# First block of a spectral filter: direct products on array quarters, halved start products, and a new order of the first loads and weight conversions

## The chip, the cores and the metric

The kernel runs on one core of a Trainium2 chip. The metric is the device time of one execution in microseconds (us). Three runs of the kernel before took 2608.47, 2609.06 and 2609.44 us, a median of 2609.06. PE is the matmul engine, DVE the vector engine (VectorE), ACT the scalar engine (ScalarE), POOL is GpSimd and SP the engine that issues most transfers.

## The reference

Eight sequences of 3008 tokens with 256 channels are filtered along the sequence in the frequency domain, and every token then goes through a two-layer network with a hard swish. `moe_w_in` and `moe_w_out` come as 64-bit floats, the rest as 32-bit floats.

```python
X = np.fft.rfft(x, axis=1)
Y = X * (filt_r + 1j * filt_i)[None, :, :]
y = np.fft.irfft(Y, n=3008, axis=1)
h = y.reshape(8 * 3008, 256) @ w_in            # 256 x 2048
g = h * np.clip(h + 3.0, 0.0, 6.0) / 6.0
out = g @ w_out                                # 2048 x 256
```

## The kernel before

**The filter.** 3008 is 47 x 64, and the transform is done in two stages of small products: over the 47 rows `a` for each of 64 columns `j` (stage a), then over the columns for each of 24 values `k` of the first frequency index (stage b). `f_unit` multiplies by the filter on VectorE (L561 to L563, three operations, one input of each in PSUM), `y_unit` forms real and imaginary sums (L572, L573, all in SBUF), `bi_unit` transforms back over the columns, and its results `t` are stored to the DRAM buffer `g_tmp` (`g_store`, on GpSimd's queue) and loaded again into `t4` in another layout. `n_five`, `n_unit` and, for the first block of tokens, `n_first` transform back over the rows into the ring `xn`.

**The network.** Tokens go in 47 blocks of 512 (`PAIRS` is 256: a token and its mirror image are handled as a pair), and each block takes 8 steps `p` over the hidden width. Block 0 runs plainly (`plain_up`, `plain_down`, L873 to L890); the later ones use sums of seven products, for which GpSimd forms sums of the weights (`w_sums`, L369) while block 0 runs. `relu` (L813) is on ScalarE and `hswish` (L818) on VectorE.

**The weights.** Each of 16 parts of 512 KB arrives as 64-bit words (`load_bits`, L317). `w_abs` on ScalarE (L323, L324) makes the absolute high words and floats of the low words; `w_conv` (L333, L335, L337) and `w_conv_2` (L354, L358, L361) on VectorE make 32-bit floats of them. Without `w_abs` VectorE does two operations more (L340, L349). Part 0 is converted during `a0_unit`, parts 1 to 3 are put around `n_first`, and the others, in halves, into the steps of block 0.

**The opening**, L984 to L1081, is written out by hand, and every engine keeps this order:

- SP loads sequence 0 (`x0_load`, six pieces), with the bits of part 0 after the first three of them; then filter table 0, the bits of part 1 and tables 1 to 5 (`table_load`, five transfers each, 768 KB in all); then the tables `direct` and `edge` and the bits of parts 2 and 3. `wi`, which `bi_unit` needs, goes over ScalarE's queue.
- `a0_unit`, eight times: four columns and both channel halves, eight full 112x128 by 112x128 products (L421), of whose 128 result columns 96 are used. The results are copied by ScalarE and VectorE.
- For c = 0 to 5: `b_unit` and `f_unit` for `i = 2c` and `2c + 1`, `turn(c + 1)` (transposes), `bi_unit(2c - 2)` and its store. `i` counts pairs of `k`.
- The last four `k` (units 10 and 11) are not loaded into `t4` for block 0. `direct` takes their part straight from `y`: 16 products in all (four `k`, two channel halves, two banks) over full 128 rows, against a table of 564 columns (two mirror halves of 47 for each of 6 column groups). Unit 8 is stored first by `g0_first` (L625), which takes only the rows that block 0 needs, and in full after `n_first`. `first_load` brings `k` 0 to 11 into `t4` (L663, when c is 4) and then `k` 12 to 19.
- `n_first` adds the rest into the same PSUM banks, 12 products of 94 columns in two strips each (through `strips`, L765), and ScalarE copies the result to `xn` (L741, L744, L745). Then `plain_up(0)` begins.

Tiles rotate. Those that matter here: units 0, 4 and 8 and the `y` of the last units take turns in the two `t1` buffers, so the copies of unit 8 wait until unit 4's store has landed; units 2, 6 and 10 share one `t3` buffer.

Of the kernel before, what the change touches and what calls it, by code (L numbers as in the profile page):

```python
# [27 lines left out]
NA = 47  # L28
# [27 lines left out]
ND = (NJ + 1) * TOK  # L56
NX = PAIRS - NJ * NA
# [21 lines left out]
def _make_tables():  # L79
# [65 lines left out]
    def first_of(x, n):  # L145
        if n < NJ:
            return np.concatenate(x)
        return np.concatenate([x[0][:NX], x[1][:NX], cs_of([x[0][NX:], x[1][NX:]])])

# [4 lines left out]
    first = np.zeros((P, NJ + 1, TOK))  # L154
    last = np.zeros((P, NJ + 1, TOK))
    direct = np.zeros((P, TC, ND))
    for k in range(KH):
        for j in range(HC):
            for (ri, hh), x in terms(k, j, rows).items():
                if j in FIRST:  # L160
                    first[hh * 64 + ri * 32 + k, FIRST.index(j)] = first_of(x, FIRST.index(j))
                if j < 2:
                    ones[ri * ATOM + hh * KH + k, j] = cs_of(x)
# [3 lines left out]
            if j > 1:  # L167
                c, s = (terms(k, j, rows)[0, hh][0] for hh in range(2))
                for hh, v in enumerate((c, s)):
                    groups[hh * KH + k, j] = groups[HALF + hh * KH + k, j] = v  # L170
        if k >= KH - TC:
            for q in range(64):
                fr = k + NA * q if q < 32 else NA * (q - 31) - k
                for n, j in enumerate(FIRST):
                    th = [2 * np.pi * ((fr * rows(j, h, a)) % N) / N for h in range(2)]
                    direct[q, k - KH + TC, n * TOK:(n + 1) * TOK] = 2 / N * first_of(np.cos(th), n)
                    direct[HALF + q, k - KH + TC, n * TOK:(n + 1) * TOK] = -2 / N * first_of(np.sin(th), n)
    wai = np.concatenate([t.reshape(P, -1) for t in (groups, ones, first, last)], axis=1)
# [5 lines left out]
def kernel(  # L184
# [22 lines left out]
    g_d = nc.dram_tensor("g_tmp", (B, NC, 2, KH, D), FP32, kind="Internal").ap()  # L207

# [99 lines left out]
    def w_load(i, q):  # L308
        if W_AT[i] == "g":
            t = gp.tile([P, 7, 256], FP32, name="g")  # L310
            st["rest"] = t[:, 4:7, :].rearrange("p a n -> p (a n)")
# [8 lines left out]
    def w_abs(i):  # L320
        words = st["bits", i].rearrange("p (n two) -> p n two", two=2)
        st["high", i] = sp.tile([P, 512], FP32, name="s1")
        nc.scalar.activation(out=st["high", i], in_=words[:, :, 1].bitcast(FP32), func=AXT.Abs)  # L323
        nc.scalar.activation(out=words[:, :, 0].bitcast(FP32), in_=words[:, :, 0].bitcast(mybir.dt.uint32), func=AXT.Copy, scale=2.0 ** -32)  # L324


    def w_conv(i):
# [11 lines left out]
        if ("high", i) not in st:  # L339
            v.tensor_scalar(out=lo, in0=lo, scalar1=9, scalar2=0x3F800000,  # L340
                            op0=ALU.logical_shift_right, op1=ALU.bitwise_or)

# [74 lines left out]
    def a0_unit(j):  # L417
        for dh in range(2):
            ps = bank(0)
            for u in range(4):  # L420
                nc.tensor.matmul(ps[:, ts(u, P)], x0[0:XR, j + u, ts(dh, P)], st["start"][0:XR, ts(1, P)],  # L421
                                 start=True, stop=True)
            copy(dh and j not in (8, 12), zt(dh).rearrange("p (n j) -> p j n", j=HC)[:, j:j + 4, :],
# [197 lines left out]
    def g0_first(i):  # L621
        t = st["t3", 0, i]
        for v in range(2):
            for h in range(2):
                (nc.scalar, nc.sync)[v].dma_start(g_d[0, ds(h * HC + 1, NJ + 1), :, ds(2 * (i + v), 2), :].rearrange("c ri u d -> c ri (u d)"),  # L625
                                    t[ds(v * 64 + h * HC + 1, NJ + 1)].rearrange("p ri u d -> p ri (u d)"))
# [32 lines left out]
    def first_load(k0, k1):  # L659
        for h in range(2):  # L660
            for ri in range(2):
                p0 = h * 64 + ri * 32
# [59 lines left out]

    def direct(i):
        if "psn" not in st:
            st["psn"] = {(c, dh): (psO.tile([P, 2, 2, P], FP32, name="po%d" % (2 + dh)).rearrange("p a u m -> p (a u m)")
                                   if c else psF.tile([P, 512], FP32, name="psn", tag="f"))
                         for c in range(2) for dh in range(2)}
        for u in range(2):
            k = 2 * i + u - KH + TC
            for (c, dh), ps in st["psn"].items():  # L730
                t, n = c * NJ * TOK, (1 if c else NJ) * TOK
                nc.tensor.matmul(ps[:, 0:n], st["y", 0, i][:, u, ts(dh, P)], st["direct"][k][:, ds(t, n)],
                                 start=k == 0, stop=False, skip_group_check=True)

    def n_first():
        for (c, dh), ps in st.pop("psn").items():
            for q, j in enumerate(chunks[c][1]):
                strips(ps[:, ts(q, TOK)], t4[:, j - 1, ts(dh, P)], edges[:, FIRST.index(j), :], start=False, stop=True)
            to = xn[:, dh, :, 0:PAIRS]
            if c == 0:  # L740
                nc.scalar.activation(out=to[:, :, 0:NJ * NA].rearrange("p h (j a) -> p j h a", a=NA),  # L741
                                     in_=ps[:, 0:NJ * TOK].rearrange("p (j h a) -> p j h a", j=NJ, h=2), func=AXT.Copy)
                continue
            nc.scalar.activation(out=to[:, :, NJ * NA:], in_=ps[:, 0:2 * NX].rearrange("p (h a) -> p h a", h=2), func=AXT.Copy)  # L744
            nc.scalar.activation(out=xn[:, dh, :, ds(PAIRS, NA - NX)],  # L745
                                 in_=ps[:, 2 * NX:TOK].rearrange("p (c a) -> p c a", c=2), func=AXT.Copy)
# [233 lines left out]
    with tc.manual_schedule():  # L980
# [42 lines left out]
        nc.scalar.dma_start(wi, wi_d)  # L1023
# [7 lines left out]
        for j, n, bits in (0, 4, 0), (4, 4, 0), (8, 8, 1), (16, 8, 1), (24, 4, 1), (28, 4, 1):  # L1031
            x0_load(j, n)
            load_bits(bits)
        table_load(0, 0)
        load_bits(2)
        table_load(0, 1)
        for j in range(0, HC, 4):
            a0_unit(j)
            convert(j == 4)
        nc.gpsimd.memset(t4, 0.0)  # L1040
# [249 lines left out]
```

## Time and profile before

| | us |
|---|---|
| median of three runs | 2609.06 |
| profiled execution, first to last instruction (span) | 2607.0 |
| median of the runs above the span | 2.06 |
| PE busy | 2591.8 (99%) |
| VectorE busy | 2053.9 (79%) |
| ScalarE busy | 1295.6 (50%) |
| GpSimd busy | 486.7 (19%) |

The profiled execution's own time is known by its span; what lies outside of it is taken from the timed runs. The granted clock of PE is 1.000 in the mean. Some places of the opening, from the timeline and the records of transfers:

| what | us |
|---|---|
| first and last product of `a0_unit` begin | 6.6 to 21.8 |
| first `f_unit` begins | 25.36 |
| last `y_unit` ends | 54.65 |
| stores of units 0, 2, 4 and 6 issued | 33.3, 38.0, 42.65, 48.5 |
| bits of part 3 (last of the first loads) landed | 50.16 |
| `direct` on PE | 51.13 to 59.7 |
| last load of `first_load` landed | 61.53 |
| first product of `n_first`, of `plain_up(0)`, of `plain_up(1)` | 61.62, 64.22, 68.55 |
| VectorE's conversion of part 3 begins, idles, goes on | 62.36, 64.03, 65.64 |

How to read it: in the timeline a line has start, length, engine, line of the kernel, operation, what is written and read, and in square brackets how long the engine stood idle before it and what ended that. In the groups the number after the bar is busy time, then the mean ns of one instruction, then idle time. The slices cut the span into 40 pieces of 65 us, in tenths busy. The chain of waits gives start, length and what ran. One product of 32-bit floats is two weight loads and two matmul instructions, so ten products in two strips are 40 instructions.

### The profile page before, as it was taken

The numbers are of one execution on the slowest core, as the hardware profiler recorded it, in microseconds if no ns is written. First come the engines' busy times: TensorE is split into PE (matmuls) and PEld (weight loads), VectorE is DVE, ScalarE is ACT, GpSimd is POOL, SyncE is SP. The second block draws the span as 40 slices with busy tenths as digits, with TensorE's granted clock in tenths as the row PEclk, the third lists the DMA queues.
The fourth block names the chain that finished last, engine by engine and source line by source line (L and its number), as shares of the span: only waits on it lengthen the run. The fifth ranks groups of instructions, "written<-read, shape, count | busy, mean of one in ns | idle before, by whom it ended". The sixth has DMA issues, their size and how long they took to land.

```text
span 2607.0 us, 86613 instructions
## 1 busy us (share of the span) xinstructions
PE 2591.8 (99%) x37708; PEld 2051.0 (79%) x37708; DVE 2053.9 (79%) x3611; ACT 1295.6 (50%) x2677; POOL 486.7 (19%) x711
## 2 busy tenths in 40 slices
PE   8999999999999999999999999999999999999999
PEld 6487777878778787788877888777877778888887
DVE  7978868888788877888778887788877888766666
ACT  4554454545545455444554444545445454455554
POOL 2242021121211202111031210311113120111110
PEclk9999999999999999999999999999999999999999
DMA  8732234112241132411224112331123321110000
GB/s 247 224 92 81 59 101 119 54 33 87 74 123 54 33 87 78 119 54 37 83 83 114 54 38 82 89 108 54 54 66 91 106 57 49 50 44 24 20 22 26
DMA packets 130834, 200.32 MB, mean 77 GB/s; under 512 B 21602, under 2 KB 97472, under 8 KB 130262
## 3 DMA queue, kind: packets, MB, share of 16 engines
q1 hardware_dynamic: 115165, 150.12, 20.4%
q0 software_dynamic: 14720, 44.16, 6.1%
q8 instruction: 296, 4.85, 0.8%
q14 instruction: 84, 0.69, 0.1%
q10 hardware_dynamic: 569, 0.50, 0.1%
HBM read 122.43 MB, written 83.98 MB: 79 GB/s over the span
## 4 chain that ended last, share of the span: by engine, by line
PE 94%; DVE 3%; DMA 2%; POOL 1%; issue 0%; ACT 0%; SPq 0%; POOLq 0%; DVEq 0%; ACTq 0%
PE po L765 43%; PE al L765 24%; PE be L765 18%; PE psn L705 2%; PE psf L540 1%; PE psf L481 1%; PE psf L600 1%; PE be L600 1%; POOL w_all L369 1%; PE be L481 1%; DVE g L818 1%; DMA g_tmp<-t 1%; PE psf L765 0%; DMA ft<-in_filt_i_dram 0%; DVE y L335 0%
## 5 line engine op out<-in xcount | busy, mean ns | idle before, releaser
L765 PEld LDWEIGHTS po<-w_all,g 128*64 128x64 f32 x20808 | 1232.5, 137 | 247.0 <-issue 12.4
L765 PE MATMUL po<-w_all,g 128*64 128x128 f32 (+1 forms) x20808 | 1407.0, 274 | 1.4 <-DVE g L818 0.7
L813 ACT ACTIVATE r<-h,half_c 128x512 f32<-128x512 f32 x736 | 531.0, 722 | 346.7 <-DVE h L794 334.7
L765 PE MATMUL al<-xt,w_all 128*64 128x256 f32 x4416 | 664.0, 379 | 0.4 <-POOL w_all L369 0.3
L818 DVE SCALAR_TENSOR_TENSOR g<-r,h 128x512 f32<-128x512 f32 x736 | 536.2, 730 | 144.6 <-ACT r L813 129.2
L765 PE MATMUL be<-xt,w_all 128*64 128x256 f32 x2944 | 442.6, 379 | 0.0
L794 DVE TENSOR_TENSOR h<-be,s 128x512 f32<-128x512 f32 x368 | 253.8, 690 | 131.3 <-PE be L765 102.2
L760 POOL TENSOR_TENSOR xt<-xn 128x256 f32<-128x256 f32 x184 | 150.7, 838 | 890.3 <-ACT xn L687 890.3
L765 PEld LDWEIGHTS be<-xt,w_all 128*64 128x64 f32 x2944 | 211.3, 137 | 106.5
L765 PEld LDWEIGHTS al<-xt,w_all 128*64 128x64 f32 x4416 | 278.9, 137 | 1.7 <-POOL w_all L369 1.4
L808 ACT ACTIVATE h<-al 128x256 f32<-128x256 f32 x368 | 141.4, 384 | 273.2 <-PE al L765 272.4
L826 DVE TENSOR_TENSOR g<-g 128x512 f32<-128x512 f32 x367 | 261.4, 712 | 12.6
L799 DVE TENSOR_TENSOR h<-al,s 128x256 f32<-128x256 f32 x368 | 156.0, 424 | 135.6 <-PE al L765 130.5
L789 ACT ACTIVATE s<-al 128x256 f32<-128x256 f32 x368 | 141.6, 385 | 207.2 <-PE al L765 207.1
L765 PE MATMUL al<-xn,w_all 128*64 128x256 f32 (+1 forms) x1536 | 240.1, 393 | 1.1 <-DVE g L818 0.7
L765 PE MATMUL be<-xn,w_all 128*64 128x256 f32 (+1 forms) x1536 | 236.4, 388 | 0.0
L780 ACT ACTIVATE s<-be 128x256 f32<-128x256 f32 x368 | 141.4, 384 | 170.1 <-PE be L765 170.1
L825 DVE TENSOR_TENSOR g<-g 128x256 f32<-128x256 f32 x367 | 165.5, 451 | 12.6
L779 ACT ACTIVATE s<-al 128x256 f32<-128x256 f32 x368 | 141.5, 384 | 59.1 <-PE al L765 59.1
L831 DVE TENSOR_TENSOR g<-g 128x256 f32<-128x256 f32 x367 | 161.7, 441 | 2.4
L765 PEld LDWEIGHTS be<-xn,w_all 128*64 128x64 f32 x1536 | 110.3, 137 | 62.3 <-issue 7.4
L506 POOL DMA_DIRECT2D z_tmp<-t x144 | 72.0, 508 | 321.4 <-ACT s L780 296.0
(162 smaller groups left out, 1766.6 us busy)
## 6 DMA issues: line engine op xcount, KB each, us to landing
t<-g_tmp SPq DMA_DIRECT2D x184, 120.0 KB
t<-z_tmp SPq DMA_DIRECT2D x42, 512.0 KB
g_tmp<-t POOLq DMA_DIRECT2D x68, 256.0 KB, 4.3
z_tmp<-t POOLq DMA_DIRECT2D x120, 144.0 KB, 3.7
o_tmp<-o SPq DMA_DIRECT2D x46, 256.0 KB
xs<-in_x_dram SPq DMA_DIRECT2D x60, 192.0 KB
ft<-in_filt_r_dram SPq DMA_DIRECT2D x168, 64.0 KB
ft<-in_filt_i_dram SPq DMA_DIRECT2D x168, 64.0 KB
```

What stands on the lines that cost most here:

```text
L760: nc.gpsimd.tensor_tensor(out=o, in0=x0, in1=x1, op=op_)
L765: nc.tensor.matmul(ps[ds(o, STRIP)], w[:, ds(o, STRIP)], x, skip_group_check=True, **kw)
L779: nc.scalar.activation(out=s[:, 0, :], in_=al, func=AXT.Copy)
L780: nc.scalar.activation(out=s5, in_=be[:, 1, :], func=AXT.Copy)
L789: nc.scalar.activation(out=s[:, 1, :], in_=al, func=AXT.Copy)
L794: nc.vector.tensor_tensor(out=st["h"][0].rearrange("p (a n) -> p a n", a=2), in0=be, in1=s, op=ALU.add)
L799: nc.vector.tensor_tensor(out=st["h"][1][:, 256:512], in0=al, in1=s5, op=ALU.add)
L813: nc.scalar.activation(out=r, in_=st["h"][i], func=AXT.Relu, bias=half_c, scale=1.0 / 6.0)
L818: nc.vector.scalar_tensor_tensor(out=st["g", k, p][:, o:o + 2, :].rearrange("p a n -> p (a n)"), in0=st["r", i], scalar=1.0, in1=st["h"][i ...
L825: v.tensor_tensor(out=g[:, G1, :], in0=g[:, G3, :], in1=g[:, G22, :], op=ALU.add)
L826: v.tensor_tensor(out=g[:, G3:G2 + 1:2, :], in0=g[:, G3:G1 + 1, :], in1=g[:, G11:G11 + 1, :].broadcast_to([P, 2, 256]), op=ALU.subtract)
L831: nc.vector.tensor_tensor(out=g[:, G4, :], in0=g[:, G12, :], in1=g[:, G2, :], op=ALU.subtract)
```

## The change

It has five parts, all before block 0 or in it.

1. `a0_unit` computes 96 instead of 128 columns, in two strips of 64 weight columns. VectorE now copies every second group.
2. On SP, all of x comes first, then tables 0 and 1, bits 0, `wi` (moved from ScalarE's queue), tables 2 and 3, bits 1, tables 4 and 5, then the tables of `direct` and `n_first` and bits 2 and 3.
3. Parts 0 and 1 are converted at c = 1 and c = 3: `w_abs` on ScalarE, the first half on VectorE and the second half, four operations, on GpSimd (`w_conv_2g`), ahead of the stores of units 0 and 4 in GpSimd's queue. Part 2 comes ahead of `n_first`, part 3 after it.
4. `direct` and `n_first` compute even and odd sums: real and imaginary rows are separate 64-row products of 47 instead of 94 columns per group, on four quarters of the array. Sum and difference are taken by VectorE in `n_first`. The table has 282 columns for each `k` (564 KB for four instead of 1128 KB), and `n_first` reads the six column groups of `groups` that it needs (141 KB, loaded ahead of the rest of `wai`) instead of a table `first` of its own (282 KB), which goes.
5. Units 6 and 8 go to block 0 through a DRAM buffer of their own, `gf_tmp` (`gf_store`, `gf_load`); unit 6 is stored to `g_tmp` as well, unit 8 as before after `n_first`. Only the part of `t4` that block 0 reads is cleared.

```diff
+NE = (NJ + 1) * NA
...
-            if j > 1:
+            if j:
...
+                    th = 2 * np.pi * ((fr * rows(j, 0, a)) % N) / N
+                    direct[q, k - KH + TC, n * NA:(n + 1) * NA] = 2 / N * np.cos(th)
+                    direct[HALF + q, k - KH + TC, n * NA:(n + 1) * NA] = 2 / N * np.sin(th)
...
+    gf_d = nc.dram_tensor("gf_tmp", (2, HC + NJ + 1, 2, TC, D), FP32, kind="Internal").ap()
...
-    def w_abs(i):
+    def w_abs(i, early=False):
         words = st["bits", i].rearrange("p (n two) -> p n two", two=2)
-        st["high", i] = sp.tile([P, 512], FP32, name="s1")
+        st["high", i] = rp.tile([P, 512], FP32, name="r", tag="r") if early else sp.tile([P, 512], FP32, name="s1")
...
+                             scale=2.0 ** (-52 if early else -32))
...
+    def w_conv_2g(i):
+        big, rest, lo, _ = st.pop(("conv", i))
+        rest, big, high, g = rest.bitcast(FP32), big.bitcast(FP32), st.pop(("high", i)), nc.gpsimd
+        two = lambda t: t.rearrange("p (a d) -> p a d", a=2)
+        g.tensor_tensor(out=rest, in0=lo.bitcast(FP32), in1=rest, op=ALU.mult)
+        g.tensor_tensor(out=rest, in0=rest, in1=big, op=ALU.add)
+        g.tensor_scalar(out=high, in0=high, scalar1=1.125 * 2.0 ** -15, scalar2=None, op0=ALU.is_ge)
+        g.tensor_tensor(out=w_part(i)[1], in0=two(high), in1=two(rest), op=ALU.mult)
...
-                nc.tensor.matmul(ps[:, ts(u, P)], x0[0:XR, j + u, ts(dh, P)], st["start"][0:XR, ts(1, P)],
-                                 start=True, stop=True)
-            copy(dh and j not in (8, 12), zt(dh).rearrange("p (n j) -> p j n", j=HC)[:, j:j + 4, :],
+                strips(ps[:, ds(u * P, 4 * KH)], x0[0:XR, j + u, ts(dh, P)], st["start"][0:XR, ds(P, 4 * KH)],
+                       start=True, stop=True)
+            copy(dh, zt(dh).rearrange("p (n j) -> p j n", j=HC)[:, j:j + 4, :],
...
+    def gf_store(i, qs):
+        t = st["t3", 0, i]
+        for v in range(2):
+            qs[v].dma_start(gf_d[i // 2 % 2, :, :, ds(2 * v, 2), :].rearrange("c ri u d -> c ri (u d)"),
+                            t[ds(v * 64 + 1, HC + NJ + 1)].rearrange("p ri u d -> p ri (u d)"))
+
+    def gf_load(i, qs):
+        for h in range(2):
+            for ri in range(2):
+                qs[h].dma_start(t4[ds(ri * HALF + h * KH + 2 * i, TC), 0:NJ + 1, :],
+                                gf_d[i // 2 % 2, ds(h * HC, NJ + 1), ri, :, :].rearrange("j k d -> k j d"))
...
+    def quarters(ps, dh, w, x, **kw):
+        for g in range(2):
+            for c in range(2):
+                nc.tensor.matmul(ps(c, dh)[ts(g, HALF)], w(c, ds(dh * P + g * HALF, HALF)), x(c), **kw)
+
     def direct(i):
...
+            for dh in range(2):
+                quarters(lambda c, dh: ps[c][dh][:, 0:NE], dh, lambda c, m: y[ts(c, HALF), u, m],
+                         lambda c: st["direct"][ts(c, HALF), ts(k, NE)], start=k == 0, stop=False, skip_group_check=True)
 
     def n_first():
...
+        for dh in range(2):
+            for q, j in enumerate(FIRST):
+                quarters(lambda c, dh: ps[c][dh][:, ts(q, NA)], dh, lambda c, m: t4[ds(c * HALF, ATOM), j - 1, m],
+                         lambda c: groups[ds(c * HALF, ATOM), j, :], start=False, stop=True, skip_group_check=True)
+            e, o = (xn[:, dh, c, :] for c in range(2))
+            odd = ps[1][dh]
+            nc.scalar.activation(out=e[:, 0:NE], in_=ps[0][dh][:, 0:NE], func=AXT.Copy)
+            nc.vector.tensor_tensor(out=o[:, 0:PAIRS], in0=e[:, 0:PAIRS], in1=odd[:, 0:PAIRS], op=ALU.add)
+            nc.vector.tensor_tensor(out=e[:, 0:PAIRS], in0=e[:, 0:PAIRS], in1=odd[:, 0:PAIRS], op=ALU.subtract)
+            nc.scalar.activation(out=o[:, PAIRS:NE], in_=odd[:, PAIRS:NE], func=AXT.Copy)
...
-        nc.scalar.dma_start(wi, wi_d)
...
-        for j, n, bits in (0, 4, 0), (4, 4, 0), (8, 8, 1), (16, 8, 1), (24, 4, 1), (28, 4, 1):
+        for j, n in (0, 4), (4, 4), (8, 8), (16, 8), (24, 4), (28, 4):
             x0_load(j, n)
-            load_bits(bits)
         table_load(0, 0)
-        load_bits(2)
         table_load(0, 1)
+        load_bits(1)
+        nc.sync.dma_start(wi, wi_d)
         for j in range(0, HC, 4):
             a0_unit(j)
-            convert(j == 4)
-        nc.gpsimd.memset(t4, 0.0)
+        nc.gpsimd.memset(t4[:, 0:NJ + 1, :], 0.0)
         for c in range(FB, NT):
             table_load(0, c)
...
+            load_bits(1 + (c > FB))
+        st["direct"] = x0_at(HC * D - 2048, TC * NE)
+        nc.sync.dma_start(st["direct"], direct_d.rearrange("p k n -> p (k n)"))
+        nc.sync.dma_start(wai[:, NA:NA + NE], wai_d[:, NA:NA + NE])
         load_bits(3)
...
+            if c in (1, 3):
+                w_abs(done, True)
+                w_conv(done)
+                w_conv_2g(done)
+                done += 1
             if c + 1 < NT:
                 turn(c + 1)
             if c:
                 bi_unit(0, 2 * c - 2)
-                (g0_first if c == NT - 1 else lambda i: g_store(0, i))(2 * c - 2)
-            if c == 4:
+            if c == NT - 2:
+                gf_store(NU - 6, (nc.sync, nc.sync))
+                g_store(0, NU - 6)
                 first_load(0, KH - 3 * TC)
-        first_load(KH - 3 * TC, KH - TC)
-        for i in 1, 2:
-            w_abs(i)
+            elif c == NT - 1:
+                gf_store(NU - 4, (nc.sync, nc.scalar))
+            elif c:
+                g_store(0, 2 * c - 2)
+        gf_load(NU - 6, (nc.sync, nc.sync))
+        gf_load(NU - 4, (nc.sync, nc.gpsimd))
+        w_abs(2)
         direct(NU - 2)
         direct(NU - 1)
...
+        convert(1)
         n_first()
...
-        convert(3)
+        convert(1)
```

## The prediction

> **What bounds the kernel now.** I read the busy slices first, then the chain of work that ended last, then its pieces and the timeline of the first 140 us. The slices say that only the opening is open to this change: after it PE is busy without a break.
>
> ```profile
> PE   8999999999999999999999999999999999999999
> DVE  7978868888788877888778887788877888766666
> POOL 2242021121211202111031210311113120111110
> DMA  8732234112241132411224112331123321110000
> ```
>
> The chain up to the first token block (start, length, what) runs through transfers. First, loads queue up to 27.5 us; later the first block's results go out to g_tmp and come back into t4 before the first n_first product can run at 61.62.
>
> ```profile
> 1.68 8.04 DMA w_all<-in_x_dram
> ...
> 9.73 9.32 DMA ft<-in_filt_i_dram
> ...
> 19.06 8.45 DMA wa<-wb_t
> ...
> 42.65 0.53 POOL g_tmp L631
> 43.18 6.58 DMA g_tmp<-t
> ...
> 50.98 4.56 DMA g_tmp<-t
> ...
> 55.56 2.31 DMA g_tmp<-t
> ...
> 58.19 3.34 DMA t<-g_tmp
> ```
>
> Then, from 68.64 to 120.46, every piece of the chain is VectorE, and after it GpSimd's weight sums. VectorE stands still for only 2.36 us between its first f_unit (25.36) and the last conversion on the chain: 0.29 at 42.5, 0.46 at 47.0 and 1.61 at 64.03.
>
> ```profile
> 65.64 0.69 DVE L354 TENSOR_TENSOR y<-g,y 128x512 f32<-128x512 f32 x1 [1.61 <-ACT g L324]
> ...
> 119.77 0.69 DVE L361 SCALAR_TENSOR_TENSOR w_all<-s,y 128x512 f32<-128x512 f32 x1
> ```
>
> PE has no gap over 0.15 us from 68.55 to 139 but 0.67 at 96.5; its start at 68.55 is released by hswish, which stands in the same VectorE queue. So both lines move together, by as much as VectorE reaches "convert part 3" earlier. Before, that conversion starts at 62.36 and loses 1.61: its effective start is **63.97**. The forecast is a new value for this point.
>
> **a0 and x.** The 64 full products of L421 took 15.48 us, 0.242 each. They become strips of 64 x 96 columns. The nearest row is the 94-column strips: 40 instructions, ten products, in 1.85 us, 0.185 each.
>
> ```profile
> L421 PE MATMUL po<-p,w_all 112*128 112x128 f32 x128 | 15.5, 286 | 0.0
> L765 PE MATMUL psn<-wai,t 128*64 128x94 f32 x40 | 1.8, 246 | 0.8 <-DMA t<-g_tmp 0.8
> ```
>
> 64 x 0.185 = 11.84, so a0 gives back **3.64** (bounds: 5.2 if it scaled with columns to 0.16, 0 if PE waits for x). x's pieces landed at 5.47, 6.65, 9.71, 14.48, 15.83 and 17.36; the bits between took 2.05 of that (11.76 - 9.71), so the last lands at about 15.0 and is needed at 17. PE's order holds. ACT and VectorE copies (0.85 and 0.83 per 1.48 us of PE) fit. Behind x, table 0 took 2.75 us and lands near 17.7 (needed 20.6). Table 1, at the 220 GB/s of 20 to 27 us, lands at 21 to 23 (needed 23.6); bits 0 and wi follow at 25 and 25.5, wi needed at 26.5. Thin covers: each us beyond them costs at most one, and VectorE, not PE, sets the next steps. f_unit 0 then starts at 25.36 - 3.64 = 21.72.
>
> **VectorE from there.** One f_unit is 2.145 us (25.36 to 27.51), three operations of 0.69. First halves of conversions (L333, 335, 337: 0.43 + 0.75 + 0.43 and gaps) are 1.65. Eight f_units and conversion 0: 21.72 + 17.2 + 1.65 = 40.55; conversion 1 to 42.2; four f_units (8.6) and two y_units (2.85): 53.65, against 54.65 before. Conversion 2 (3.75) ends at 57.4. The two w_abs (1.35 each) hide on ScalarE, which idles 1.8 us in every step of the c loop; bits 1, behind table 3, land near 34 and are needed at 40. w_abs 2 now stands behind ScalarE's half of gf_store 8, whose issue took 0.74 to 1.34: it is done near 55.3, just when L354 wants it; another us there would cost nothing, as VectorE idles later.
>
> **GpSimd.** Each early conversion is three tensor_tensor and one tensor_scalar of 512 elements, which this trace does not show on GpSimd. The rows (min/median/max ns):
>
> ```profile
> L760 POOL TENSOR_TENSOR xt<-xn x184: 720/732/1243, 97.7 to 2531.0; 128x256 f32<-128x256 f32 x184
> L369 POOL TENSOR_TENSOR w_all<-w_all x64: 448/460/945, 120.6 to 157.1; 128x128 f32<-128x128 f32 x64
> ```
>
> 0.46 for 128 and 0.73 for 256 extrapolate to 1.28 for 512; the compare lies between a memset (2.23 for 2560, so 0.45) and 1.28, I take 0.9: **4.7 us** in all. Bounds 4.3 and 9.9 (4 x 2 x 1.243). I take the low end since the slow ones stand beside VectorE operations that read SBUF alone: L358 took 1.10 instead of 0.69 at 98.99, but the PSUM-reading L794 never more than 0.695, and the f_units read PSUM.
>
> ```profile
> 98.99 1.10 DVE L358 SCALAR_TENSOR_TENSOR y<-y 128x512 f32<-128x512 f32 x1
> ```
> ```profile
> L794 DVE TENSOR_TENSOR h<-be,s x368: 676/692/695, 130.0 to 2594.9; 128x512 f32<-128x512 f32 x184
> ```
>
> The Trainium skill, "SBUF — State Buffer", section "SBUF: two separate sides", speaks against work on GpSimd: the two engines share one pair of ports under an exclusive lock, which a VectorE operation with two SBUF inputs needs for its whole length. The two rows above agree with it, and by it the f_units stay free, since one input is PSUM; were they held as L358 is, two conversions would cost VectorE some 3.5 us (an estimate: 9.4 us at 0.69 for 1.10) and the sum would be a loss of 2.
>
> What is queued behind: g_store 0 waits for conversion 0 (31.95 + 4.7, instead of 33.3; nobody needs it before 48); g_store 2 follows it at 37.8, where it was issued at 37.98; g_store 4 waits for conversion 1: 42.2 + 4.7 = **46.9**, where it was issued at 42.65.
>
> **The way through DRAM.** GpSimd's stores landed 2.9 / 6.8 / 9.7 us (min, median, max) after issue. The one issued at 48.5, when the loads had ended, had its second half down 4.95 later; the quiet minimum gives 0.55 + 2.9. With 0.7 MB less to load (direct table 564 for 1128 KB, n_first's table 141 for 282) the queue is empty by about 47.5 instead of 50.16, so I take 4.5: down at 51.4. That releases both first_load and, by the buffer it shares, bi_unit 8's copies (to 52.6). SP issues four loads (1.8) to 53.2, then its half of gf_store 8, down 2.3 later (55.55 to 57.87 before) plus 0.4 for six times the bytes: 55.9. gf_load 8 took 3.2 before (57.88 to 61.07): rows complete at **59.1**, where they were at 61.53. The GpSimd half of gf_load, two issues of 0.6 on a queue idle by then, has a landing of 2.9 at least: the same within 0.6. gf_store 6 and gf_load 6 lie earlier on SP and beside these waits. The halved memset of t4 (2.23 to 1.34) runs where GpSimd idles. SP holds an issue until the landing of one eight places before (the piece at 9.73 waited for 9.71); in this stretch those are short transfers, and I count nothing, with 1 us as the other end.
>
> **direct and n_first.** direct was 8.6 us of PE (51.13 to 59.7). The quarter row is n_five: 80 instructions in 1.31, 0.131 per product of 47 columns. 8 products of 282 columns are between 3.8 (four quarters at full rate) and 6.3 (0.131 x 6 x 8); with 4.2, PE is done with bi_unit 10 at 56.8, before the rows, so this saves nothing by itself; its cover is 2.3 us. n_first: 0.8 per half (24 / 40 of 1.31), 0.2 to drain, then ScalarE's copy of 282 columns (0.40, between 0.384 for 256 and 0.57 for 470), then VectorE's four sums at 0.43: they are new on VectorE, and convert part 3 and both hswish of the first plain step are queued behind them. 59.1 + 0.8 + 0.2 + 0.4, two sums, 0.1 for the second copy, two sums: **62.3**, rounded up to 62.5 for the queue's own gaps.
>
> **Sum.** 63.97 - 62.5 = 1.45 us earlier. A check from the work: start -3.64, work +1.65 - 2.1 + 1.75 = +1.3 (conversion 0's half, conversion 1's second half, sums), idle 3.1 (57.4 to 60.5) instead of 2.36, +0.7: -1.6. From there on nothing differs but 0.14 MB of loads. Span 2607.0 - 1.4 = 2605.6; the median of the three runs lies 2.06 above the span, so **2607.6**. A gain under 5.2 us (0.2%) cannot be told from no change here.
>
> **Rivals.**
> Rows arrive early (0.25). Quick stores (2.9), or a0 at 0.16: VectorE's 3.1 us of idle goes, at most 4.6 with this a0 (2604.5), and 1.6 more with the fast one (2602.9). For it: the queues are empty then. Against: four transfers in a row.
> The opening keeps its pace (0.15). Loads, not PE, set f_unit 0 at 25.36: everything is 3.64 later than my line, 2611.2. For: the chain's first three pieces are DMA. Against: 1.0 MB moved behind what is needed first.
> GpSimd holds the stores (0.11). At P us per conversion the end moves by P - 4.7, and twice as fast above 8, when conversion 1 waits for conversion 0. From P = 6.2 the change loses, from about 9.6 it is slower by over 0.2%: 2615 at 9.8. For: the maximum row. Against: the f_units read PSUM.
> Quarters do not run side by side (0.03): 64 passes one after another, 15 us for 4.2, 2614. Against it stands the n_five row.
>
> **Numbers.** My line 0.46. Faster by over 0.2%: 0.16 (two thirds of the first rival, beyond 2603.8); slower by over 0.2%: 0.11 (0.09 of the third rival and 0.02 of the last, beyond 2614.3); the rest within, 0.73. The range of 2602.9 to 2612.8 goes from the first rival's end, past the second rival, by the 1 us of SP's wait and a little of the table's, and leaves out the last two.
>
> **What would show it.** a0 in 11.8 us, f_unit 0 near 21.7; GpSimd operations near 1.3 us; g_store 4 issued near 47; n_first's first product near 59; VectorE idle 3 us ahead of the sums; plain_up 1 near 67.1 instead of 68.55; the VectorE chain's end near 119. It is wrong if bits or wi hold VectorE or ScalarE before 30 us, or if a DMA wait of SP ahead of gf_load shows up.

## The result and the profile after

The changed kernel takes **2625.98 us** (median of 4 runs, 2625.29 to 2627.09) beside 2608.76 for the kernel before on the same chip. The ratio is 1.007, with a 95% interval from 1.0058 to 1.0081: slower by 0.7%. The forecast was 2607.6 with a range of 2602.9 to 2612.8, so it was wrong by 18 us and the time lies outside of the range. The span of the profiled execution is 2624.2, 17.2 more than before.

The busy slices of the changed kernel show where the time is: for PE only the first two of them have changed (7 and 8 for 8 and 9), and VectorE has less to show in the same two (6 and 7 for 7 and 9). GpSimd has more to do in the first.

```profile
PE   7899999999999999999999999999999999999999
DVE  6778967888778887788868888688877888766666
POOL 3161113111121111211122111211112110111110
DMA  8742234212342123421224212241133421210000
```

The point on which the forecast rested was the effective start of VectorE's conversion of part 3, 63.97 before. It is now 81.21: 17.24 later, and the span is 17.2 longer. So the frame held, and all of the error lies ahead of 81.21. The chain of waits of the first 90 us (start, length, what) names what lies there:

```profile
50.40 3.95 DMA g_tmp<-t
...
55.56 10.33 DMA gf_tmp<-t
...
65.91 4.09 DMA t<-gf_tmp
...
70.78 6.10 DMA t<-gf_tmp
...
81.21 0.43 DVE y L327
```

A store of 152 KB takes 10.33 us, where the store of 24 KB to g_tmp that stood in this place took 2.31. The loads behind it take 4.09 and 6.10, where the last one took 3.34. VectorE stands still meanwhile (timeline; in brackets the idle time before):

```profile
78.92 0.42 DVE L757 TENSOR_TENSOR xn<-xn,po 128x256 f32<-128x256 f32 x1 [18.60 <-ACT xn L756]
```

The table by stretches of 2 us shows what kind of wait it is. Its columns are the stretch and its length, busy time of PE, PEld, DVE, ACT and POOL, then PE's granted clock, the share of the 16 DMA engines that is busy, and GB/s:

```profile
60.00:62.00 2.00, 1.70 (x24) 0.56 (x16) 0.33 (x1) 0.00 (x0) 0.00 (x0) 1.00 0.13 50
62.00:64.00 2.00, 0.00 (x0) 0.00 (x0) 0.00 (x0) 0.00 (x0) 0.00 (x0) 1.00 0.13 49
...
66.00:68.00 2.00, 0.00 (x0) 0.00 (x0) 0.00 (x0) 0.00 (x0) 0.00 (x0) 0.58 0.19 69
68.00:70.00 2.00, 0.00 (x0) 0.00 (x0) 0.00 (x0) 0.00 (x0) 0.00 (x0) 0.50 0.12 45
```

From 62 to 70 us all five engines wait for DMA, but for two copies on ScalarE, and the DMA engines are almost idle too: a share of 0.13 is 2 of 16. 50 GB/s by two is 25 GB/s for each. That is no busy queue. It is a transfer that may use only two engines. The four stores `gf_store` were issued at 50.41, 51.28, 55.56 and 58.25 and landed at 59.14, 64.34, 65.89 and 69.46, some 8.7 to 13 us after their issue, one behind the other. The records of their landings agree. On SP's and ScalarE's queues a transfer of 128 rows leaves 16 records of completion in these traces, a load of 12 rows 13 and a store of 6 rows 7, so one more than engines where these are fewer than 16; each of these stores leaves 3, one of them 1.1 to 1.4 us after the issue and two late. Each moves 38 rows, and 38 is 2 x 19. The two engines held other transfers too: the four loads of 12 rows by `first_load`, issued at 54.49 to 57.58, had ten of their twelve pieces down by 56.75 to 60.31 and the last two only at 63.92 to 66.44, among the landings of the stores.

The Trainium skill, "DMA: Bandwidth & Descriptors", section "Why a DMA increments its semaphore by 16 and not by 1", has the rule: a transfer is spread over the largest number of engines up to 16 that divides the slowest dimension of both sides. For 38 rows that is 2, which is what the share of 0.13 shows. The prediction made no use of it.

### The profile page after: what moved, and what is told of

Its sections match the earlier page's. It is cut to its first block, busy times and chain, and to the rows that moved or that the text cites. A ratio compares the mean times of both kernels' runs of the same rounds, so it can differ in the third digit from the quotient of the medians.

```text
span 2624.2 us, 87050 instructions
## 1 busy us (share of the span) xinstructions
PE 2588.5 (99%) x37916; PEld 2046.1 (78%) x37916; DVE 2052.0 (78%) x3609; ACT 1294.9 (49%) x2675; POOL 498.5 (19%) x721
## 4 chain that ended last, share of the span: by engine, by line
PE 95%; DMA 2%; DVE 1%; issue 0%; POOL 0%; ACT 0%; POOLq 0%; SPq 0%; DVEq 0%; ACTq 0%
PE po L778 44%; PE al L778 25%; PE be L778 18%; PE psn L713 2%; PE psf L543 1%; PE psf L484 1%; PE psf L603 1%; PE be L603 1%; PE be L484 1%; DMA ft<-in_filt_i_dram 0%; DMA gf_tmp<-t 0%; DMA t<-gf_tmp 0%; PE psf L778 0%; PE psf L457 0%; DMA wi<-wi_t 0%
## 5 line engine op out<-in xcount | busy, mean ns | idle before, releaser
L792 ACT ACTIVATE s<-al 128x256 f32<-128x256 f32 x368 | 141.5, 384 | 59.1 <-PE al L778 59.1
```

Of the source, the lines that this page charges most:

```text
L792: nc.scalar.activation(out=s[:, 0, :], in_=al, func=AXT.Copy)
```

## The experiments

Three reasons were possible for the slow way through `gf_tmp`: (1) the row count of the stores, (2) their bytes or the traffic beside them, (3) GpSimd's part, as loader of two of the four pieces and as the queue in which the stores of units 0 and 4 wait behind conversions. Further kernels leave out or move parts of the change to find what each part is worth.

**All 64 rows.** More bytes, but a row count that 16 divides; the loads take the same rows from their new place in `gf_tmp`.

```diff
-    gf_d = nc.dram_tensor("gf_tmp", (2, HC + NJ + 1, 2, TC, D), FP32, kind="Internal").ap()
+    gf_d = nc.dram_tensor("gf_tmp", (2, NC, 2, TC, D), FP32, kind="Internal").ap()
...
-                            t[ds(v * 64 + 1, HC + NJ + 1)].rearrange("p ri u d -> p ri (u d)"))
+                            t[ts(v, 64)].rearrange("p ri u d -> p ri (u d)"))
...
-                                gf_d[i // 2 % 2, ds(h * HC, NJ + 1), ri, :, :].rearrange("j k d -> k j d"))
+                                gf_d[i // 2 % 2, ds(h * HC + 1, NJ + 1), ri, :, :].rearrange("j k d -> k j d"))
```

> Only change to the kernel after: gf_store sends all 64 rows of a half (256 KB instead of 152 KB) to gf_tmp. Theory 1 (38 rows go to two of the 16 DMA engines, which then work alone at 50 GB/s): each gf_store reports all 16 completions and lands within 5 us of its issue although it carries more bytes; the last one near 61.5 instead of 69.48, n_first begins near 66 instead of 75.23, and the time falls by 10 to 14 us to about 2614. Theory 2 (the stores wait behind other traffic, or it is the bytes): they land no earlier, 256/152 later at worst, and the time stays at 2626 or goes up to 2632. Either way conversion of part 3 begins as much earlier as the time falls.

Measured: 2618.05 us, ratio 1.004 [1.0025, 1.0055]. The stores land 3.1 to 6.5 us after issue, the last at 60.52 instead of 69.46, though each moves 256 KB instead of 152. This refutes the bytes. Some 4 us of the gain that I had expected are missing, and in this run the two loads on GpSimd's queue land last. In the timeline of GpSimd the loads are issued 8.9 us earlier than in the changed kernel:

```profile
61.18 1.25 POOL L633 DMA_DIRECT2D t<-gf_tmp  x2 [9.21 <-DMA t<-gf_tmp]
62.42 2.37 POOL L639 DMA_DIRECT2D g_tmp<-t  x4
```

They land at 65.79 and 67.81, 4.6 and 6.0 us after issue, while SP's two, of the same 24 KB and issued 0.3 to 0.6 us ahead of them, landed at 62.82 and 63.29, after 2.2 and 2.4.

**Forty rows.** The same kernel with 160 KB for each store instead of 152, so that bytes are almost equal and only the divisors differ.

```diff
-    gf_d = nc.dram_tensor("gf_tmp", (2, HC + NJ + 1, 2, TC, D), FP32, kind="Internal").ap()
+    gf_d = nc.dram_tensor("gf_tmp", (2, HC + NJ + 3, 2, TC, D), FP32, kind="Internal").ap()
...
-                            t[ds(v * 64 + 1, HC + NJ + 1)].rearrange("p ri u d -> p ri (u d)"))
+                            t[ds(v * 64, HC + NJ + 3)].rearrange("p ri u d -> p ri (u d)"))
...
-                                gf_d[i // 2 % 2, ds(h * HC, NJ + 1), ri, :, :].rearrange("j k d -> k j d"))
+                                gf_d[i // 2 % 2, ds(h * HC + 1, NJ + 1), ri, :, :].rearrange("j k d -> k j d"))
```

> The changed kernel with one size altered: gf_store moves 40 rows (0 to 39) of each half instead of 38 (1 to 38), so 160 KB for 152 KB, 5% more. gf_tmp has 40 rows, the loads are the same six. If the row count decides how many of the 16 DMA engines a store is spread over (38 = 2 x 19 on two, 40 = 4 x 10 = 5 x 8 on eight or ten), then each of the two engines of the changed kernel moved 25 KB/us (50 GB/s between 60 and 70 us), 160 KB on eight need 0.8 us besides the latency, the four stores land 2.5 to 5 us after issue instead of 8.7 to 13, and the time is that of the kernel with 64 rows or a little less: 2616 to 2618.5. The rival, that the stores are slow by their bytes, by the DRAM layout or by what else moves at the time: landings of 8 us and more stay, and the time is 2625 to 2627.

Measured: 2618.57 us, ratio 1.0041 [1.0026, 1.0056]. The stores land 3.2 to 6.7 us after issue, the last at 60.91, and each leaves 11 records of completion, so ten engines. In the same table by stretches the DMA share is 0.56 and 0.61 while these stores run; the loads of 12 rows are in it too, so it is not a measure of the stores alone:

```profile
56.00:58.00 2.00, 2.00 (x40) 1.28 (x36) 1.59 (x3) 0.50 (x2) 0.00 (x0) 1.00 0.56 168
58.00:60.00 2.00, 2.00 (x36) 1.08 (x28) 1.15 (x2) 0.78 (x2) 0.00 (x0) 1.00 0.61 198
```

Two rows more are worth 7.4 us. That settles it for the first reason, the row count.

**Six rows.** Each store as two pieces of six rows, 24 KB each, on SP and ScalarE.

```diff
-            qs[v].dma_start(gf_d[i // 2 % 2, :, :, ds(2 * v, 2), :].rearrange("c ri u d -> c ri (u d)"),
-                            t[ds(v * 64 + 1, HC + NJ + 1)].rearrange("p ri u d -> p ri (u d)"))
+            for h in range(2):
+                qs[v].dma_start(gf_d[i // 2 % 2, ds(h * HC, NJ + 1), :, ds(2 * v, 2), :].rearrange("c ri u d -> c ri (u d)"),
+                                t[ds(v * 64 + h * HC + 1, NJ + 1)].rearrange("p ri u d -> p ri (u d)"))
```

> Only change to the kernel after: each gf_store half becomes two transfers of the six rows each that block 0 needs (24 KB each, as g0_first of the kernel before had them), over six engines by the completions that g0_first showed. Theory 1 (too few engines): landing within 2.3 to 4.5 us of the issue, the time about 2613, at or a little below the version with all rows, since four short issues more on SP (0.4 to 0.9 each) stand against fewer bytes. Theory 2 (other traffic in the way): a landing of 8 to 11 us as before, and 2624 or more.

Measured: 2619.01 us, ratio 1.0042 [1.0027, 1.0057]. The pieces go to six engines and land after 2.2 to 5.3 us, but there are twice as many issues of 0.73 to 1.33 us each, the last lands at 62.24, and GpSimd's loads land at 67.21 and 69.60. So the stores did what the first reason says, and the time falls by 7.0 us; the 2613 that I had expected is missed, with the issues and GpSimd's loads behind the stores.

**All loads on SP.** Only the two loads move from GpSimd to SP; the stores stay at 38 rows.

```diff
-        gf_load(NU - 4, (nc.sync, nc.gpsimd))
+        gf_load(NU - 4, (nc.sync, nc.sync))
```

> Only change to the kernel after: the two loads of unit 8 that GpSimd issued are issued by SP, ahead of the bits of parts 4 and 5. If the GpSimd queue is what made the last two loads land at 75.14 and 76.89 (5.0 and 6.1 us after issue, beside the bulk loads), n_first begins near 73 and the time falls by 3 to 4.5 us to about 2622. If the two-engine stores are all of it, it falls by under 1 us. The gf_store landings stay at 8 to 13 us in both.

Measured: 2625.73 us, ratio 1.0069 [1.0054, 1.0084], a span of 2623.5: 0.7 less. The stores still land 9.3 to 15.4 us after issue. The last one lands at 72.40, 2.9 us later than in the changed kernel, so the run does not tell what the loads' queue is worth by itself: the next one shows what else moved.

**All 64 rows and all loads on SP.** Both edits at once.

> The kernel after with all 64 rows in gf_store and the last two loads on SP. Theory 1a (once the stores land in time, the GpSimd queue is the next loss: in the run with all rows its two loads landed at 65.80 and 67.82, SP's at 63.31): the last load lands near 64, conversion of part 3 begins near 68.3 instead of 72.15, and the time is 2613 to 2615. Rival (these loads are no later than what SP would do, since bits of parts 4 and 5 then come behind them and delay something else): 2617 or more.

Measured: 2617.6 us, ratio 1.0036 [1.0023, 1.0049]. I had expected 2613 to 2615, and this part of my theory fell. GpSimd's wait for its loads had also held the full store of unit 8, which stands behind them in its queue. Without it that store is issued at 56.54 (at 56.29 in the run before), and its traffic runs beside SP's transfers: the last `gf_store` is issued at 59.35 instead of 57.38, and the last load lands at 68.22. So what the loads gained by their queue was lost again, by my reading to the store that was let go; no run keeps that store back with all loads on SP, so this is argued and not shown.

**The old route.** Units 6 and 8 go through `g_tmp` again, with `first_load` and `g0_first` as before; parts 1 to 4 of the change stay.

```diff
-            if c == NT - 2:
-                gf_store(NU - 6, (nc.sync, nc.sync))
-                g_store(0, NU - 6)
+            if c:
+                (g0_first if c == NT - 1 else lambda i: g_store(0, i))(2 * c - 2)
+            if c == 4:
                 first_load(0, KH - 3 * TC)
...
-        gf_load(NU - 6, (nc.sync, nc.sync))
-        gf_load(NU - 4, (nc.sync, nc.gpsimd))
+        first_load(KH - 3 * TC, KH - TC)
```

> Parts 1 to 4 of the change with the old way through DRAM (g0_first for unit 8, g_store for unit 6, first_load of 12 to 19, no gf_tmp). If the new buffer's transfers are the whole loss, the rest of the change is worth what my line said less its 2 us late start: conversion of part 3 begins at 65 to 67 and the time is 2609 to 2613. If the delayed stores behind GpSimd's conversions are a loss of their own, unit 6's store (issued at 50.95, landed at 58.4 in the kernel after) holds the second first_load until 59 and n_first until 63 to 65, and the time is 2612 to 2615.

Measured: 2611.81 us, ratio 1.0015 [1.0005, 1.0024]. The last load lands at 63.57 and the conversion of part 3 starts at 67.37. So part 5 of the change costs 14.2 of the 17.2 us, some 8 by the two engines and some 6 by its other transfers. The 3.4 that are left beside the kernel before on the same chip (2608.45) must lie in parts 1 to 4.

**The old route, stores first.** The suspect for them: the stores of units 0 and 4 stand behind conversions in GpSimd's queue. Here the conversions are issued behind those stores.

```diff
             if c in (1, 3):
                 w_abs(done, True)
                 w_conv(done)
-                w_conv_2g(done)
-                done += 1
...
+            if c in (1, 3):
+                w_conv_2g(done)
+                done += 1
```

> Parts 1 to 4 with the old route, and GpSimd's half of the early conversions put behind the stores of units 0 and 4 in its queue, nothing else moved. Theory 3 (what is left of the loss, 3.4 us, comes from stores waiting behind conversions on GpSimd): unit 4's store is issued near 41.5 instead of 49.52, first_load near 49 instead of 54.52, conversion of part 3 begins at 63 to 64.5 instead of 67.38, and the time is 2607 to 2609.5. Rival (the later f_units, 1.65 us of VectorE work added twice, set the end): the conversion begins at 66 or later, 2611 or more.

Measured: 2609.26 us, ratio 1.0003 [0.9995, 1.0012], no more to be told from the kernel before. The timeline of GpSimd shows the order turned round:

```profile
41.22 1.13 POOL L633 DMA_DIRECT2D g_tmp<-t  x2 [0.51 <-ACT t L589]
44.40 1.30 POOL L340 TENSOR_TENSOR y<-bits,y 128x512 f32<-128x512 f32 x1 [2.04 <-DVE y L330]
```

Unit 4's store goes at 41.22 instead of 49.5, the last load lands at 59.24 instead of 63.57, and the conversion of part 3 starts at 64.12, close to the 63.97 of before.

**The strips alone.** The kernel before with part 1 only, `a0_unit` in strips of 96 columns.

```diff
-                nc.tensor.matmul(ps[:, ts(u, P)], x0[0:XR, j + u, ts(dh, P)], st["start"][0:XR, ts(1, P)],
-                                 start=True, stop=True)
+                strips(ps[:, ds(u * P, 4 * KH)], x0[0:XR, j + u, ts(dh, P)], st["start"][0:XR, ds(P, 4 * KH)],
+                       start=True, stop=True)
```

> The kernel before with only the products of a0_unit as strips of 96 columns; order of loads, copies and conversions as before. If a0 on PE is worth something by itself, f_unit 0 begins at 22.5 to 24 instead of 25.36 (x's last piece lands at 17.4 and holds a0 until 19) and the time falls by 1 to 2.5 us to about 2606.5. If the loads through g_tmp and their queue set the end whatever PE does, or the pieces of x hold a0 until 21, it stays within 0.7 us of before.

Measured: 2609.23 us, ratio 1.0004 [0.9995, 1.0013]. The first f_unit begins at 25.92, no earlier than 25.36. With the old order of the loads x sets the pace: PE stands for 2.31 us until a piece of it lands and goes on at 15.64. Then its granted clock is 0.50 from 15.33 to 18.74, so the last product of `a0_unit` begins at 22.38, where it began at 21.8 before.

**All three at once for the changed kernel.** 64 rows, loads on SP, stores ahead of the conversions.

> The kernel after with three things mended: all 64 rows in gf_store, all gf_load on SP, GpSimd's conversions behind the stores of units 0 and 4. If these three are the whole of the loss, the last load lands near 58.5, conversion of part 3 begins at 62 to 63, and the time is 2606.5 to 2608, 1 us below the kernel before or equal to it. If it begins later than 65, something else in the change costs, and the old route is the better one.

Measured: 2611.68 us, ratio 1.0015 [1.0006, 1.0024], against an expectation of at most 2608. The full stores of units 6 and 8, 512 KB each, issued at 49.84 and 50.96 and down at 55.78 and 58.39, now run beside the `gf_store` of unit 8 (50.41 and 52.61, landed at 57.66 and 59.14). The last load lands at 62.47, 3.2 later than on the old route, which sends unit 8's rows in pieces of 24 KB and its full store only at 59.79.

**Idle time ahead of the sums.** Two more kernels, on the old route with stores first, try to use the 1.97 us for which VectorE still waits ahead of the sums of `n_first`: the first half of part 3's conversion goes there.

```diff
         convert(1)
+        w_abs(3)
+        w_conv(3)
         n_first()
...
-        w_abs(3)
-        convert(1)
+        w_conv_2(done)
+        done += 1
```

> The kernel with the old route and the stores first (2609.26, VectorE idle 1.97 and 0.62 us around the sums of n_first), with the first half of part 3's conversion (w_abs on ScalarE, three operations of 1.61 us on VectorE) ahead of n_first instead of behind it. Theory: what sets the end is VectorE's queue up to the conversions, so every idle us filled ahead of the sums is gained: the half fits in the 1.97 us, the second half of the conversion begins at 64.3 instead of 65.9, and the time is 1.6 us less, 2607.4 to 2608.2; beside the kernel before that is 0.9995 to 1, not to be told from it. Rival: n_first on PE sets the pace and the idle time moves to where the next token step waits for PE; then no change, 2609 to 2609.6. A loss, 2611 or more, if the two buffers of the second half wait for the conversion before them.

Measured: 2610.79 us, ratio 1.0009 [1.0, 1.0018]. Here `w_abs` stood in ScalarE's queue ahead of the copies that the sums wait for, so the run does not answer its question. Behind `w_abs` of part 2, where ScalarE idles, it does:

```diff
         w_abs(2)
+        w_abs(3)
         direct(NU - 2)
...
         convert(1)
-        w_abs(3)
         w_conv(3)
         n_first()
```

> The run before put part 3's w_abs into ScalarE's queue ahead of n_first's copies, which it held up by 1.2 us (first copy at 63.32 instead of 61.39, of which 0.7 is the run's later start). Here w_abs of part 3 stands right behind w_abs of part 2, where ScalarE idles 6 us, and the first half of its conversion stands ahead of n_first as before. Theory (VectorE's queue sets the end): the sums begin at 61.9 as in the kernel with the stores first, the second half begins at 64.2 instead of 65.9, hswish follows without a gap, and the time is 2607.4 to 2608.2. Rival (the first plain step on PE and ScalarE sets the end): VectorE stands idle ahead of the two hswish, 1.6 us in sum, and the time is 2609 to 2609.8.

Measured: 2607.82 us, ratio 0.9998 [0.9989, 1.0007]. VectorE waits 1.53, 0.62 and 1.03 us around the sums although 1.6 us of work was put in:

```profile
63.61 0.42 DVE L751 TENSOR_TENSOR xn<-xn,po 128x256 f32<-128x256 f32 x1 [1.53 <-PE po L728]
```

`n_first` itself had become late: the sums begin 4.2 us after the last load has landed (59.42), where it was 2.6 in the run with the stores first. (The profiled execution, 2609.49 us, is the longest of the eleven; its last product of `a0_unit` begins at 20.77, 0.6 later than there.) The reason is in the table by stretches, in the column before the last but one, PE's granted clock:

```profile
54.00:56.00 2.00, 0.98 (x8) 0.55 (x12) 1.92 (x4) 1.56 (x3) 0.00 (x0) 0.50 0.21 66
...
58.00:60.00 2.00, 2.00 (x24) 1.10 (x20) 1.83 (x4) 0.00 (x0) 0.03 (x1) 0.50 0.96 236
```

**PE kept busy.** The same with products that nobody reads in PE's idle time ahead of `bi_unit` 8 and of `direct`.

```diff
+                nc.tensor.matmul(ps[:, 0:256], wi.rearrange("p a n -> p (a n)")[:, 0:P], wi.rearrange("p a n -> p (a n)"), start=True, stop=True)
...
+            if c == NT - 1:
+                ps = psU.tile([P, 512], FP32, name="al")
+                fill(2)
...
+        fill(4)
         direct(NU - 2)
+        fill(3)
         direct(NU - 1)
```

> The run before, with idle PE time in front of direct filled by products that nobody reads (64-bank tables of wi, 256 columns: two ahead of bi_unit 8, four ahead of direct's first, three ahead of its second half; some 0.43 us each). Without them the granted clock stood at 0.50 from 54 to 60 us, the quarter groups of direct took 0.47 us instead of 0.24 to 0.27, direct ended at 60.2 and n_first's first sum began at 63.6, 4.2 after the last load (59.43). Theory: the clock is taken back because PE stood idle, 0.4 to 1.4 of each 2 us from 50 to 56; filled, the granted clock stays at 1.00, the groups take 0.24 to 0.27, direct ends near 57.6, n_first starts with the last load, the sums begin 2.3 us behind it, at 61.7 to 62, and VectorE's wait of 1.5 ahead of them is gone: 2606.3 to 2607 (beside the kernel before about 0.9992, at the edge of what can be told). Rival: the clock falls for another reason (the form of the products on 64 rows and quarters), the granted clock stays at 0.50 there and the time at 2607.8; or the fillers delay direct, 2609.

Measured: 2607.39 us, ratio 1.0 [0.9991, 1.0009]. The theory of the clock is right: it stays at 1.00 in the same stretches,

```profile
54.00:56.00 2.00, 2.00 (x24) 1.20 (x25) 1.84 (x4) 0.48 (x1) 0.00 (x0) 1.00 0.13 43
...
58.00:60.00 2.00, 2.00 (x45) 1.11 (x40) 1.93 (x4) 0.00 (x0) 0.55 (x2) 1.00 1.02 335
```

and VectorE's wait ahead of the sums falls to 0.46:

```profile
61.42 0.42 DVE L751 TENSOR_TENSOR xn<-xn,po 128x256 f32<-128x256 f32 x1 [0.46 <-PE po L728]
```

The span of the profiled execution, 2605.4, is 1.6 below that of before, but the kernel before has spans of 2604.9 to 2606.9 on this run's chip, and the timed runs can't tell the two from each other. No kernel here beats the one before by more than the measurement can tell.

## Why the prediction was wrong

**The step that failed** is the one that read "SP issues four loads (1.8) to 53.2, then its half of gf_store 8, down 2.3 later (55.55 to 57.87 before) plus 0.4 for six times the bytes: 55.9". The stores measured 8.7 to 13 us, and the last was down at 69.46. The nearest row was a piece of six rows, on six engines; I scaled its bytes and took its number of engines for granted. The whole path was then "rows complete at 59.1" and measured 76.88. What was wrong was the rate. Behind it GpSimd's loads of unit 8 took 5.0 and 6.1 us beside the bits of the next parts, issued at 70.16; they took 4.6 and 6.0 beside them in the run with 64 rows too, so this is not a price of being late.

Point by point, with the number of the prediction first:

- **The frame**: effective start of part 3's conversion plus 2543 us is the span. Right: this difference is 2542.98 before and 2542.95 after, and 2542.6 to 2543.5 in the runs above that keep the order of VectorE's queue.
- **Strips**: 0.185 us each, 11.84 in all. Right in price. The groups by line give 12.1, and the timeline of PE shows what came in between:

```profile
13.24 3.85 PE L778 MATMUL po<-p,w_all 112*64 112x96 f32 x88 [0.18 <-DMA w_all<-in_x_dram]
18.50 1.87 PE L778 MATMUL po<-p,w_all 112*64 112x96 f32 x40 [1.40 <-issue]
```

x's last piece landed at 16.55, not 15.0 (17.36 less the 2.05 of the bits would have been 15.3). But PE did not wait for it: it stands for 1.40 us ahead of 18.50, within the seventh `a0_unit`, whose products had begun. It stands there for 1.2 to 1.7 us, ahead of the same product, in each profile that has the new order of loads, and the profile names nothing that releases it. So f_unit 0 begins at 23.66 instead of 21.72, and of the 3.64 us only 1.7 came. The cause is open, and no run changes it. What the traces have is a transfer of 16 KB on an instruction queue that ends at 17.01 in the changed kernel; in all twelve profiles PE goes on 1.3 to 1.6 us after the end of this transfer. With the strips and the old order it ends at 17.16, PE comes to the same product only at 20.79, and does not stop. This suggests that PE's instructions came too late for the faster PE.
- **VectorE's line**: last y_unit at 53.65, measured 55.74. Right, with the 2 us of the start. The f_units' operations take 0.68 to 0.70 beside GpSimd's work, as I took from the row whose input is in PSUM.
- **GpSimd**: 4.7 us for a conversion; the second one begins at 44.41 and its store is issued at 49.81, 5.4 later, with the three tensor_tensor as extrapolated (1.28) and the compare above its bound, 1.49 for 1.28:

```profile
44.41 1.30 POOL L341 TENSOR_TENSOR y<-bits,y 128x512 f32<-128x512 f32 x1 [2.37 <-ACT t L418]
45.79 1.27 POOL L342 TENSOR_TENSOR y<-y 128x512 f32<-128x512 f32 x1
47.03 1.49 POOL L343 TENSOR_SCALAR r<-r 128x512 f32<-128x512 f32 x1
48.60 1.26 POOL L344 TENSOR_TENSOR w_all<-r,y 128x512 f32<-128x512 f32 x1
49.81 2.36 POOL L639 DMA_DIRECT2D g_tmp<-t  x4
```

- **Unit 4's store**: issued at 46.9, down 4.5 later. The 4.5 is right (49.81 to 54.34), the issue 2.9 late. I saw this store wait and priced it, and yet set the rival "GpSimd holds the stores" to begin at 6.2 us for each conversion. On the old route the order alone is worth 2.5 us (2611.81 to 2609.26), with conversions of 5.4. My reading of the gap: the store's wait counts in full where the line has no slack left, and the late start had used it up.
- **gf_load 8**: 3.2 for SP's part and 2.9 at least for GpSimd's. SP's took 2.3, GpSimd's 5.0 and 6.1. That the row is a minimum was said; the median of the same rows, 6.8, was not kept in the range.
- **direct**: 4.2 us of PE. In the last kernel, at full clock, its three stretches have 4.9 (four quarter products start together every 0.23 to 0.29 us, so the rival that they run one after another is out). In the changed kernel PE ran most of it at a granted clock of 0.52 to 0.63. No term for the clock was in the sum, since the granted clock is 1.00 there before.
- **The rivals**: none of them was what came, though half of one (the opening keeps its pace: 2 of its 3.64 us) and a part of another (GpSimd holds the stores) are in the sum. All took the transfers as short; the one wait that I named for SP had 1 us. The last rival's 2614 does not follow from its own numbers: 10.8 us more on PE, less the cover of 2.3, on 2607.6 is 2616.

The whole of the 17.2 us then is: some 8 from stores on two engines, some 6 from the other transfers of the new route (its loads on GpSimd's queue, or the full stores that run beside it instead), 2.5 from stores behind conversions. These are differences between runs (2625.98, 2618.05, 2611.81, 2609.26), made on several chips, on which the kernel before took 2608.09 to 2608.76, and how the 6 divides among loads and stores was not separated.

## What to carry to other kernels

Ask of every new transfer over how many engines it is spread, before its bytes: count the completion records of the nearest row, and look at the factors of its row count (38 rows cost 8.7 to 13 us where 40 cost 3.2 to 6.7). A transfer on a waiting path is priced with its queue: what stands ahead of it, and what its wait holds back that will run beside it once it is let go. An engine that was made faster than its loads gained nothing here, and by idling it lost its clock (the strips alone).

## What the runs showed of the hardware

- **38 rows went over two DMA engines** (share 0.13, 50 GB/s, 3 completion records), 40 rows over ten (11 records), 64 rows over 16 (16 records). Loads that share the two engines waited there behind the stores: ten of twelve pieces were down after 2.3 to 4.0 us, the last two after 8.3 to 11.2.
- **PE's granted clock falls to 0.50 though no single gap is long.** In the kernel with `w_abs` moved PE stood for 1.84 us at 50.4 and for 1.44 at 53.6, with 1.4 us of work in between, and ran from 54 to 60 at half clock: a quarter product of 282 columns took 0.67 us instead of 0.40. Fillers kept the clock at 1.00. In the clock records of the fourteen profiles a state lasts a multiple of 3.41 us. Taken over stretches of this length, PE was busy for at most 49% in each of the 34 ahead of a fall, and the clock stayed at 1.00 behind some 10,600 others, of which two had less than 49% (43% and 48%). The Trainium skill, "TensorE: Matmul & The Clock Gate", section "What's actually happening", gives one idle window of about 3.4 us as the condition. The length agrees with these records, but the gaps here are shorter and PE was at work for part of the window, so there the measurement decides.
- **Loads of 24 KB on GpSimd's queue landed 4.3 to 6.1 us after issue** in the changed kernel and those with 64, 40 and six rows; SP's last two, of the same size and issued just ahead of them, after 2.2 to 2.5. Bits were loaded beside the former, so the queue alone is not shown to be the reason.
- **GpSimd's compare of 512 elements takes 1.48 to 1.50 us**, longer than its tensor_tensor (1.26 to 1.31), though it has one input.
